# Convolutions of a forward and backward step moved beside the MLP matmuls, on one core

## The chip, the core and the metric

One NeuronCore of a Trainium2 chip: TensorE (PE) for matmuls into PSUM, VectorE (DVE), ScalarE (ACT) and GpSimd (POOL) for elementwise work, SyncE (SP) which issues transfers, and 16 DMA engines between HBM and SBUF. The metric is device time in microseconds of one execution, lower is better. All tensors are bf16.

## What is computed

A layer norm of x (2048 rows, 1024 channels), then two branches that are added to x: a gated convolution over the sequence and a gated MLP; and the gradients of all inputs but one for a given grad_out. Cut to what matters:

```python
xn = layernorm(q)                                   # [2048, 1024]
# branch A, per channel: a 4-tap shift, a product, a long convolution by FFT of length 4096
k_shift = sum(k_pad[:, t:t+S] * shift_k[:, 3-t] for t in range(4))
kv = k_shift * v
y  = irfft(rfft(kv, 4096) * rfft(ssm_k, 4096))[:S] + kv * ssm_D
A  = xn * y
# branch B, F = 3584
gate = xn @ W_gate;  up = xn @ W_up
h = relu(gate) * up;  B = h @ W_down
out = q + A + B
outputs = out, and vjp(grad_out) for q, k, v, shift_k, ssm_k, ssm_D, W_gate, W_up, W_down
```

The convolution needs, per channel, three forward transforms (of kv, of ssm_k, and of grad_out * xn), three products in the frequency domain, and three inverse transforms (of y, of the gradient of kv and of the gradient of ssm_k). The MLP needs nine products of 2048 x 1024 x 3584: gate, up, h W_down, grad of h, grad of W_down, grads of W_gate and W_up, and two products for the grad of xn.

## The kernel before

The program is recorded in Python, and a scheduler orders each engine's instructions by priority; engines run their own lists strictly in that order and wait for each other by semaphores. Buffers come from pools with a fixed number of buffers per name; an allocation waits until the oldest buffer of that name is free.

Stages, in the order in which they are written:

1. `_a_branch`, first part: tables of sines (R1, FW, IA, RB) on POOL, DVE and ACT. Beside it the layer norm: one load of x, sums, `xn_dram` and `gy_dram` (grad_out * xn) written.
2. `_a_branch`, first pass over eight groups of 128 channels (`A_load`, `A_part1`, `A_part2`): the taps on a channel-major copy (made by transposing DMAs), `fwd_transform` for kv, gy and ssm_k (matmuls with R1 at L299, evictions at L48, 64 matmuls of 128 columns with FW at L309 and L311), `jpass` (L320) to swap real and imaginary halves, products on DVE (L434 to L457), and a spill of three 1 MB forms to HBM.
3. Second pass over the same groups (`B_load`, `inverse_A`, `inverse_B`): reload of the forms, matmuls with IA (L335), 64 TensorE transposes a form (L345), matmuls with RB (L357), outputs.
4. Gate and up (L755, L759): xnT loaded by transposing DMAs; 7 column blocks of 512 by 16 row tiles; each step has 16 matmuls of 512 columns, a relu on ACT (L762), a masked product on DVE (L764), a product on POOL (L767), and three stores of 128 KB (SP and ACT queues).
5. Out (L806): per row tile a transposed load hT, 2 x 28 matmuls.
6. Per block of 512 hidden columns: the gradient of h (L837; two loads and two stores of 128 KB per row tile, on SP, ACT and POOL queues), and then, from SBUF, the gradients of W_gate and W_up (L853).
7. Gradient of W_down (L888); W_gate and W_up are transposed by two DMAs beside it (L881, L882).
8. Gradient of x (L924, L928): per row tile two transposed loads and 2 x 56 matmuls, then the layer norm's backward on DVE.

Transfers are issued from SP, ACT and POOL; all transposing DMAs from SP. Stage 4 starts when stage 3 is over, because `for _ in abr: pass` exhausts the branch first and its pools hold SBUF and PSUM until then:

```python
    next(abr)
    for _ in abr:
        pass
```

Of the kernel before, what the change touches and what calls it, by code (L numbers as in the profile page):

```python
# [21 lines left out]
def a_branch(tc, S, D, k, v, shift_k, ssm_k, ssm_D, gy_d, y_d, out_gk, out_gv, out_gsk, out_gh, out_gsD):  # L22
    with ExitStack() as ctx:
        yield from _a_branch(ctx, tc, S, D, k, v, shift_k, ssm_k, ssm_D, gy_d, y_d, out_gk, out_gv, out_gsk, out_gh,
                             out_gsD)


def _a_branch(ctx, tc, S, D, k, v, shift_k, ssm_k, ssm_D, gy_d, y_d, out_gk, out_gv, out_gsk, out_gh, out_gsD):
    nc = tc.nc
    N1 = S // P  # L30
    K1 = 2 * N1
    CL = P // N1
    NCH = N1
# [12 lines left out]

    def ev_act(out, in_):
        nc.scalar.copy(out=out, in_=in_)  # L48

    def ev_dve(out, in_):  # L50
        nc.vector.tensor_copy(out=out, in_=in_)

    _rr = [0]

    def ev_rr(out, in_):
        if _rr[0] % 3 == 2:
            nc.vector.tensor_copy(out=out, in_=in_)
        else:
            nc.scalar.copy(out=out, in_=in_)
        _rr[0] += 1  # L60

    tq = nc.sync
    dq = nc.gpsimd

    acon = ctx.enter_context(tc.tile_pool(name="acon", bufs=1))
    aps = ctx.enter_context(tc.tile_pool(name="aps", bufs=2, space=bass.MemoryType.PSUM))

    R1 = acon.tile([P, CL, 2, K1], BF16, name="R1")
    FW = acon.tile([P, K1, 3, 64], BF16, name="FW")
# [201 lines left out]
    def tm_view(ap2d):  # L271
        return ap2d.rearrange("(n1 n2) c -> n2 n1 c", n2=P)
# [716 lines left out]
```

## Time and profile before

| | us |
|---|---|
| timed, median of 3 | 3142.05 (3135.73 to 3146.0) |
| profiled execution, span from first to last instruction | 3167.4 |
| PE busy | 2355.5 (74%) |
| DVE busy | 1162.3 (37%) |
| ACT busy | 719.9 (23%) |
| DMA traffic | 422.90 MB, mean 134 GB/s |

The profiled execution's span lies 0.8% above the timed median. A busy PE counts matmuls that overlap, so it is not PE at its peak; how fast it works is seen from how far apart matmuls start. [...]

### The profile page before, as it was taken

Reading aid. Unit: us, or ns where it says so; the run is one execution under the profiler, and the core shown is the slowest. Engines: PE = TensorE matmul, PEld = TensorE weight load, DVE = VectorE, ACT = ScalarE, POOL = GpSimd, SP = SyncE. Lnnn points to the kernel's source line nnn. Section 1 sums busy time; section 2 is a strip of 40 time slices with the busy share of each in tenths; the row PEclk is TensorE's granted clock in tenths of the full one; section 3 lists DMA queues with packets and bytes.
Section 4 is the critical chain, followed back from the end, with each engine's and each line's share of the span. In section 5 each row is a group of like instructions: output and inputs, shape, how many; then the busy total and the mean of one; then the engine's idle time right before and its main releaser. Section 6 shows DMA issues by size and latency. Waiting matters only on the chain. (4 is left out here: it accounts for less than half of the span.)

```text
span 3167.4 us, 35589 instructions
## 1 busy us (share of the span) xinstructions
PE 2355.5 (74%) x14665; PEld 1256.9 (40%) x14850; DVE 1162.3 (37%) x1290; ACT 719.9 (23%) x623; POOL 417.4 (13%) x547
## 2 busy tenths in 40 slices
PE   0155655555555543599997997999999998999998
PEld 0033433334445443244443443444444443444443
DVE  9687565554655546111111122211112200122233
ACT  3255665653323321011110001111111100000000
POOL 1221111000000000233331001100011000111110
PEclk9978888777777776799998999999999998999999
DMA  1695331247688947844457767444454398254452
GB/s 63 207 187 128 94 99 60 92 121 108 129 117 113 135 99 101 248 151 159 142 160 204 161 159 228 127 121 113 105 136 131 122 192 209 77 125 117 113 124 63
DMA packets 695987, 422.90 MB, mean 134 GB/s; under 512 B 517264, under 2 KB 649872, under 8 KB 689680
## 3 DMA queue, kind: packets, MB, share of 16 engines
q1 hardware_dynamic: 568480, 221.32, 34.8%
q0 software_dynamic: 29008, 100.18, 10.6%
q10 hardware_dynamic: 98336, 99.13, 10.3%
q8 instruction: 116, 1.90, 0.3%
q14 instruction: 47, 0.39, 0.0%
HBM read 154.16 MB, written 158.35 MB: 99 GB/s over the span
## 5 line engine op out<-in xcount | busy, mean ns | idle before, releaser
L853 PEld LDWEIGHTS <-xn_nat 128*128 128x128 bf16 x1792 | 177.2, 99 | 238.9 <-issue 33.0
L755 PE MATMUL ps_g<-wg,xnT 128*128 128x512 bf16 x876 | 212.8, 383 | 79.6 <-issue 72.4
L48 ACT CAST cp<-psa 128x2048 bf16<-128x2048 f32 x96 | 174.0, 1873 | 366.2 <-PE psa L335 349.5
L853 PE MATMUL ps<-gg_blk,xn_nat 128*128 128x512 bf16 x879 | 210.0, 390 | 21.3 <-ACT wo L857 19.3
L888 PE MATMUL ps<-g_nat,hs 128*128 128x512 bf16 x878 | 199.6, 388 | 21.3 <-ACT wo L893 19.4
L806 PE MATMUL ps<-wd,hT 128*128 128x512 bf16 x878 | 197.5, 385 | 23.6 <-DMA hT<-h_dram 18.4
L759 PE MATMUL ps_u<-wu,xnT 128*128 128x512 bf16 x880 | 211.0, 380 | 0.9
L837 PE MATMUL ps<-wdT,goT 128*128 128x512 bf16 x877 | 198.2, 381 | 16.7 <-ACT gh L844 14.3
L764 DVE SCALAR_TENSOR_TENSOR upm<-rg,ps_u 128x512 bf16<-128x512 bf16 x112 | 76.9, 688 | 349.4 <-PE ps_u L759 318.1
L299 PE MATMUL ps<-R,xt_h 128*128 128x512 bf16 x128 | 47.5, 514 | 211.7 <-DVE xn_t L717 102.0
L48 ACT CAST bsb<-ps 128x2048 bf16<-128x2048 f32 x96 | 173.7, 1876 | 134.4 <-DVE prod L446 59.4
L853 PE MATMUL ps<-gu_blk,xn_nat 128*128 128x512 bf16 x878 | 201.4, 379 | 0.9
L924 PE MATMUL ps<-wgT,ggT 128*128 128x512 bf16 x879 | 197.5, 379 | 1.8 <-DVE wo L895 0.9
L928 PE MATMUL ps<-wuT,guT 128*128 128x512 bf16 x878 | 197.5, 379 | 0.9
L345 PE MATMUL pstr<-identb,cp 128*128 128x128 bf16 x1536 | 130.4, 267 | 66.1 <-ACT cp L48 59.0
L859 DVE CAST wo<-ps 128x512 bf16<-128x512 f32 x56 | 38.7, 692 | 364.8 <-PE ps L853 320.7
L309 PE MATMUL ps<-bsb,FW 128*128 128x128 bf16 x768 | 130.5, 270 | 55.9 <-ACT bsb L48 55.9
L755 PEld LDWEIGHTS <-xnT 128*128 128x128 bf16 x896 | 88.2, 99 | 186.2 <-issue 82.4
L767 POOL TENSOR_TENSOR ht<-rg,upm 128x512 bf16<-128x512 bf16 x112 | 129.0, 1152 | 250.8 <-DVE upm L764 247.5
L762 ACT ACTIVATE rg<-ps_g 128x512 bf16<-128x512 f32 x112 | 66.8, 597 | 411.7 <-PE ps_g L755 278.5
L844 ACT CAST gh<-ps 128x512 bf16<-128x512 f32 x112 | 65.4, 585 | 399.0 <-PE ps L837 275.6
L345 PEld LDWEIGHTS <-cp 128*128 128x128 bf16 x1536 | 125.6, 124 | 70.7 <-ACT cp L48 63.2
(241 smaller groups left out, 2978.4 us busy)
## 6 DMA issues: line engine op xcount, KB each, us to landing
forms_d<-prod POOLq DMA_DIRECT2D x24, 1024.0 KB, 4.3
rg_dram<-rg SPq DMA_DIRECT2D x112, 128.0 KB, 1.8
up_dram<-upm ACTq DMA_DIRECT2D x112, 128.0 KB, 1.7
rg_t<-rg_dram ACTq DMA_DIRECT2D x112, 128.0 KB, 3.8
h_dram<-ht SPq DMA_DIRECT2D x112, 128.0 KB, 1.7
upm_t<-up_dram POOLq DMA_DIRECT2D x112, 128.0 KB, 3.5
gg_dram<-gg_blk SPq DMA_DIRECT2D x112, 128.0 KB, 3.7
gu_dram<-gu_blk ACTq DMA_DIRECT2D x112, 128.0 KB, 3.1
```

Source lines behind the costliest of these rows:

```text
L48: nc.scalar.copy(out=out, in_=in_)
L309: nc.tensor.matmul(ps2[:, j * P:(j + 1) * P], lhsT=fw[:, 0:128], rhs=bsb[:, 0, k1, :], start=True, stop=False)
L345: nc.tensor.transpose(pst[:, j * P:(j + 1) * P], cpf[:, (q + j) * P:(q + j + 1) * P], identb[:])
L755: nc.tensor.matmul(ps_g[:], lhsT=xnT[:, kt, st * P:(st + 1) * P], rhs=wg[:, kt, :], start=(kt == 0), stop=(kt == DT - 1))
L759: nc.tensor.matmul(ps_u[:], lhsT=xnT[:, kt, st * P:(st + 1) * P], rhs=wu[:, kt, :], start=(kt == 0), stop=(kt == DT - 1))
L767: nc.gpsimd.tensor_tensor(out=ht[:], in0=rg[:], in1=upm[:], op=ALU.mult)
L806: nc.tensor.matmul(ps[:], lhsT=hT[:, kt, :], rhs=wd[:, kt, ob * 512:(ob + 1) * 512], start=(kt == 0), stop=(kt == FT - 1))
L837: nc.tensor.matmul(ps[:], lhsT=goT[:, kt, st * P:(st + 1) * P], rhs=wdT[:, kt, :], start=(kt == 0), stop=(kt == DT - 1))
L853: nc.tensor.matmul(ps2[:], lhsT=xn_nat[:, skt, dc * P:(dc + 1) * P], rhs=blk[:, skt, :], start=(skt == 0), stop=(skt == ST - 1))
L888: nc.tensor.matmul(ps[:], lhsT=hs[:, skt, j * P:(j + 1) * P], rhs=g_nat[:, skt, ob * 512:(ob + 1) * 512], start=(skt == 0), stop=(skt == S ...
L924: nc.tensor.matmul(ps[:], lhsT=ggT[:, kt, :], rhs=wgT[:, kt, ob * 512:(ob + 1) * 512], start=(i == 0), stop=(i == n_mm - 1))
L928: nc.tensor.matmul(ps[:], lhsT=guT[:, kt, :], rhs=wuT[:, kt, ob * 512:(ob + 1) * 512], start=(i == 0), stop=(i == n_mm - 1))
```

## The change

The file is rewritten around two classes.

**ABranch** does the convolution. Per group of 128 channels it does everything in one pass, nothing is spilled: a sequence of 2048 is read as 128 x 16 (natural layout, 256 B pieces), the transform is a 32-point step (matmuls with R, 16 of 512 columns for two halves), a transposition of 32 x 32 blocks on DVE (`flip`), and a 64-point step (32 matmuls of 128 columns with FW). Products (`cmul`) are complex multiplications by parts on DVE. The inverse runs the same steps backwards. The taps use natural-layout rows with an offset, so the transposing DMAs of the branch are gone; the 4 x 128 sums of the shift gradient are now matmuls with a selecting matrix (`hsel`).

**LnMlp** does layer norm and MLP. The layer norm runs in chunks of 1, 1, 2, 4, 4, 4 row tiles, with sums on ACT, and transposes on PE into 16 tiles that stay in SBUF. Gate/up works on hidden blocks of 256 and pairs of row tiles: matmuls of 256 columns, two row tiles in one PSUM bank; the product that POOL did is on DVE. The order of phases is now gate/up, grad_hidden, grad_down (W_down), grad_in (W_gate, W_up), out, grad_x. grad_hidden stores its two results and grad_in loads them back in slabs of 512 KB. Out comes after grad_in; its phase also transposes W_gate and W_up, in eight slices. Tiles come from small pools shared by all phases: 16 of 2 KB, 5 of 4 KB (weights and slabs), 9 of 1 KB (steps), 4 PSUM banks; the branch has 2 x 2 banks. Every transfer is issued from SP.

The branch's instructions get priorities of their own: its matmuls and loads stand ahead of the MLP, its evictions, DVE work and stores behind it. Core of the diff:

```diff
-    next(abr)
-    for _ in abr:
-        pass
...
+PR_LN = -10_000_000
+PR_A_PE = 0
+PR_A_LD = 0
+PR_B = 10_000_000
+PR_A_EV = 20_000_000
...
+    def flip(self, src):
+
+        dst = self.big.tile([P, NB1, P], BF16, name="flp", tag="big")
+        df = dst[:].rearrange("p k c -> p (k c)").bitcast(F32).rearrange("p (k cp) -> p cp k", cp=64)
+        sf = src[:].rearrange("p cp r i -> p (cp r i)").bitcast(F32).rearrange("p (cp r) -> p cp r", cp=64)
+        for c0 in range(0, 64, 32):
+            self.pri.at(PR_A_EV)
+            self.nc.vector.transpose(out=df[:, c0:c0 + 32, :], in_=sf[:, c0:c0 + 32, :])
+        return dst
+
+    def forward(self, src, form_name, add_D=None):
+        B = self.big.tile([P, 64, NB1, 2], BF16, name="B", tag="big")
+        for u in range(2):
+            for j in range(2):
+                ps = self.ps.tile([P, 1024], F32, name="ps1", tag="aps")
+                for jj in range(2):
+                    r0 = 8 * j + 4 * jj
+                    self.mm(ps[:, 512 * jj:512 * jj + 512], self.R[:, u].rearrange("p h a k -> p (h a k)"),
+                            src[:, r0:r0 + 4, :].rearrange("p r c -> p (r c)"))
+                t0 = 16 * u + 8 * j
+                self.act(B[:, :, t0:t0 + 8, :], ps[:].rearrange("p (r cp i) -> p cp r i", r=8, i=2))
+        Bf = self.flip(B)
+        F = self.frm.tile([P, 2, 16, P], BF16, name=form_name, tag="frm")
+        for k0 in range(0, NB1, 8):
+            ps = self.ps.tile([P, 8, P], F32, name="ps2", tag="aps")
+            for j in range(8):
+                self.mm(ps[:, j, :], self.FW[:, k0 + j].rearrange("p a k -> p (a k)"), Bf[:, k0 + j, :])
...
+                for w, name in ((wg, "ps_g"), (wu, "ps_u")):
+                    ps = self.ps_tile(name)
+                    for s in range(2):
+                        xT = self.xnT[2 * sp + s]
+                        for kt in range(self.DT):
+                            nc.tensor.matmul(ps[:, s * 256:s * 256 + 256], lhsT=xT[:, kt * P:(kt + 1) * P],
+                                             rhs=w[:, kt, :], start=(kt == 0), stop=(kt == self.DT - 1))
+                    pss.append(ps)
+                rg, up, ht = self.ev_tile("rg"), self.ev_tile("up"), self.ev_tile("ht")
...
+            for sp in range(self.ST // 2):
+                rg, up = self.ev_tile("rgl"), self.ev_tile("upl")
+                fl = lambda t: t[:].rearrange("p s f -> p (s f)")
+                nc.sync.dma_start(out=fl(rg), in_=rg_d[hb, sp])
+                nc.sync.dma_start(out=fl(up), in_=up_d[hb, sp])
...
+                gh = self.ev_tile("gh")
+                nc.scalar.copy(out=fl(gh), in_=ps[:])
+                nc.vector.tensor_tensor(out=up[:], in0=gh[:], in1=up[:], op=ALU.mult)
+                nc.vector.tensor_tensor(out=gh[:], in0=gh[:], in1=rg[:], op=ALU.mult)
+                rows = slice(sp * 256, sp * 256 + 256)
+                nc.sync.dma_start(out=gg_d[rows, cols].rearrange("(s p) f -> p s f", p=P), in_=up[:])
+                nc.sync.dma_start(out=gu_d[rows, cols].rearrange("(s p) f -> p s f", p=P), in_=gh[:])
...
+            if st < 8:
+                w, wT = (Wg, self.wgT) if st < 4 else (Wu, self.wuT)
+                c = (st % 4) * 256
+                nc.sync.dma_start_transpose(out=wT[:, :, c:c + 256], in_=w[c:c + 256, :])
...
+    a.run()
+    a.close()
+    tc.cur_priority = PR_B
+    b.gate_up(B_W_gate, B_W_up, rg_d, up_d, h_d)
+    b.grad_hidden(B_W_down, g, rg_d, up_d, gg_d, gu_d)
+    b.grad_down(g, h_d, out_9)
+    b.open_right(B_W_down)
+    b.grad_in(xn_d, gg_d, gu_d, out_7, out_8)
+    b.close_left()
+    b.out_phase(x, xn_d, y_d, h_d, B_W_gate, B_W_up, out_0[0])
+    b.grad_x(g, xn_d, y_d, gg_d, gu_d, out_1[0])
```

How the instructions stand now, at three places. First PE in gate/up. Before, a run of gate or up matmuls holds nothing else (ps_g, ps_u: PSUM of gate and up):

```order
L755 LDWEIGHTS xnT
L755 MATMUL ps_g<-wg,xnT 128x512
L759 LDWEIGHTS xnT
L759 MATMUL ps_u<-wu,xnT 128x512
L759 LDWEIGHTS xnT
```

Now, in the same phase, PE goes to the first transform of kv of the first group (kvt, matrix R, L63) and back:

```order
L525 LDWEIGHTS xnT
L525 MATMUL ps_g<-wg,xnT 128x256
L63 LDWEIGHTS R
L63 MATMUL ps_780<-kvt,R 128x512
L63 LDWEIGHTS R
L63 MATMUL ps_780<-kvt,R 128x512
L525 LDWEIGHTS xnT
```

Two matmuls of the branch stand between MLP matmuls here; elsewhere some 40 MLP matmuls stand where the branch waits for a transposition on DVE; a group's 281 matmuls and transposes of the branch are spread over some 600 to 900 of the MLP.

Second, DVE in gate/up. Before, the 112 masked products are all that DVE does in the phase, and they stand in one row, between the convolution's last row and the out phase:

```order
L577 CAST gskb<-gskf 128x4
L764 SCALAR_TENSOR_TENSOR upm<-rg,ps_u 128x512 x112
L808 TENSOR_TENSOR o_12562<-ps,xa 128x512 x2
L800 TENSOR_TENSOR xa<-xa,xn_e 128x1024
L801 TENSOR_TENSOR xa<-xa,x_e 128x1024
```

Now (up and ht: the MLP's step; t, GH, flp, C: products and a transposition of the branch):

```order
L531 SCALAR_TENSOR_TENSOR up<-rg,ps_u 128x512
L71 TENSOR_TENSOR GH<-t_962 64x1024
L533 TENSOR_TENSOR ht<-rg,up 128x512
L71 TENSOR_TENSOR GH<-t_963 64x1024
L71 TENSOR_TENSOR GH<-t_962 64x1024
L71 TENSOR_TENSOR GH<-t_963 64x1024
L292 STREAM_TRANSPOSE flp<-C 128x32x32
L531 SCALAR_TENSOR_TENSOR up<-rg,ps_u 128x512
L292 STREAM_TRANSPOSE flp<-C 128x32x32
L533 TENSOR_TENSOR ht<-rg,up 128x512
```

Both the MLP's step and the branch now stand in one list, the MLP's two instructions with one to five of the branch between them.

Third, SP in the gradient of h. Before, SP holds the stores of one result (the other and the loads are on ACT and POOL) and the transposed weights:

```order
L847 DMA gg_dram<-gg_blk 128x512 x15
L827 DMA_TRANSPOSE wdT<-in_B_W_down_dram 128x8x512
L847 DMA gg_dram<-gg_blk 128x512
L861 DMA out_dram<-wo 128x512 x8
L847 DMA gg_dram<-gg_blk 128x512 x15
```

Now (rgl, upl: the loads; gg_d, gu_d: the stores; ghn: a store of the branch):

```order
L566 DMA gg_d<-upl 128x2x256
L567 DMA gu_d<-gh 128x2x256
L553 DMA rgl<-rg_d 128x512
L554 DMA upl<-up_d 128x512
L553 DMA rgl<-rg_d 128x512
L554 DMA upl<-up_d 128x512
L553 DMA rgl<-rg_d 128x512
L554 DMA upl<-up_d 128x512
L83 DMA out_dram<-ghn 128x2048
L566 DMA gg_d<-upl 128x2x256
L549 DMA_TRANSPOSE wdT<-in_B_W_down_dram 128x8x256
L567 DMA gu_d<-gh 128x2x256
```

Loads and stores of three steps alternate in one list, with the branch's stores and the transposed weights between them.

## Rows read from the trace of the kernel before

**Rows 1.** The page: busy tenths of PE in 40 slices of the span.

```profile
PE   0155655555555543599997997999999998999998
```

**Rows 2.** Busy time by stretch: from:to, length, engines (instructions), granted clock, DMA share, GB/s.

```profile
165.00:680.00 515.00, 294.19 (x2097) 187.35 (x2119) 334.71 (x201) 309.14 (x170) 63.61 (x109) 0.82 0.45 112
680.00:1265.00 585.00, 282.38 (x4576) 266.82 (x4575) 315.84 (x227) 174.05 (x96) 42.81 (x52) 0.75 0.71 114
...
1333.00:1722.00 389.00, 386.28 (x1764) 175.81 (x1798) 74.27 (x108) 63.23 (x106) 124.01 (x109) 1.00 0.50 158
...
2770.00:3167.00 397.00, 385.10 (x1757) 175.25 (x1792) 116.30 (x161) 0.00 (x0) 43.21 (x33) 0.99 0.44 108
```

**Rows 3.** Chain of work that ended last: start, length, engine, line, count.

```profile
2782.63 6.04 PE ps L924 x28
2794.72 6.04 PE ps L924 x28
```

**Rows 4.** Timeline of PE, first pass: start, length of one, line, shape; 16 rows left out.

```profile
412.10 0.22 PE L309 MATMUL ps<-bsb,FW 128*128 128x128 bf16 x1
...
413.05 0.22 PE L311 MATMUL ps<-bsb,FW 128*128 128x128 bf16 x1
```

**Rows 5.** Groups by line and shape, DVE: count, busy us, mean ns, idle before.

```profile
L764 DVE SCALAR_TENSOR_TENSOR upm<-rg,ps_u 128x512 bf16<-128x512 bf16 x112 | 76.9, 688 | 349.4 <-PE ps_u L759 318.1 <-ACT rg L762 15.2 <-remote 11.1
L845 DVE TENSOR_TENSOR gu_blk<-gh,rg_t 128x512 bf16<-128x512 bf16 x112 | 47.6, 425 | 139.8 <-ACT gh L844 118.7 <-DMA rg_t<-rg_dram 21.1
L457 DVE TENSOR_TENSOR prod<-prod,ptmp 64x4096 bf16<-64x4096 bf16 x8 | 18.3, 2289 | 0.3
L801 DVE TENSOR_TENSOR xa<-xa,x_e 128x1024 bf16<-128x1024 bf16 x16 | 11.0, 691 | 0.5
L411 DVE TENSOR_TENSOR kv_tm<-kshift_tm,v_tm 128x2048 bf16<-128x2048 bf16 x8 | 9.8, 1222 | 4.9 <-DMA kshift_tm<-kshT 4.7
L179 DVE TENSOR_TENSOR t<-n2v_f,m_f 128x1024 f32<-128x1024 f32 x4 | 4.8, 1211 | 0.0
```

**Rows 6.** The same view, ACT.

```profile
L693 ACT ACTIVATE sq<-d_all 128x1024 bf16<-128x1024 bf16 x16 | 16.3, 1048 | 9.6 <-DVE var_f L694 9.6
L114 ACT ACT_TABLE_LOAD x1 | 1.3, 1283 | 0.7 <-PEq L973 0.7
L48 ACT CAST sDb<-psb 128x1024 bf16<-128x1024 f32 x1 | 1.0, 1012 | 4.1 <-PE psb L256 4.1
```

**Rows 7.** Timeline of PE: first convolution matmul and first gate/up matmul.

```profile
112.34 1.01 PE L299 MATMUL ps<-R,xt_h 128*128 128x512 bf16 x2 [102.00 <-DVE xn_t L717]
1299.72 0.58 PE L755 MATMUL ps_g<-wg,xnT 128*128 128x512 bf16 x1 [72.22 <-issue]
```

**Rows 8.** Busy time by stretch (columns of rows 2), gradient of h in two blocks.

```profile
2017.00:2065.00 48.00, 46.09 (x209) 20.61 (x211) 13.55 (x34) 10.53 (x18) 8.59 (x16) 1.00 0.85 204
...
2200.00:2245.00 45.00, 41.39 (x187) 18.48 (x189) 13.20 (x34) 9.95 (x17) 8.60 (x16) 1.00 0.93 218
```

**Rows 9.** DMA issues: queue, operation, count, KB each, median us to landing.

```profile
rg_t<-rg_dram ACTq DMA_DIRECT2D x112, 128.0 KB, 3.8
gg_dram<-gg_blk SPq DMA_DIRECT2D x112, 128.0 KB, 3.7
y_dram<-y_tm POOLq DMA_DIRECT2D x8, 512.0 KB, 5.1
```

**Rows 10.** Timeline of SP's issues: start, length of the issue.

```profile
1502.38 0.34 SPq L772 DMA_DIRECT2D h_dram<-ht  x1
2548.78 43.58 SPq L881 DMA_TRANSPOSE wgT<-in_B_W_gate_dram  x1
2643.02 5.46 SPq L910 DMA_TRANSPOSE ggT<-gg_dram  x1
```

**Rows 11.** SP's waits: who waited for whom, us in total, times, longest.

```profile
SPq L290 <- PE ps L299: 259.3, 12, 46.2
SPq L366 <- PE psa L335: 147.7, 14, 47.3
```

More of the change, by code (lines that the diff above doesn't have):

```diff
@@ L726 @@
-    lnb.release()
-    next(abr)
-    for _ in abr:
-        pass
-    L, R = "left", "right"
-    gq_dma = nc.gpsimd
-    p_xnT = tc.alloc_tile_pool(name="gf_xnT", bufs=1, side=L)
-    p_w = tc.alloc_tile_pool(name="gf_w", bufs=2, side=L)
-    p_ev1 = tc.alloc_tile_pool(name="gf_ev", bufs=3, side=L)
-    p_ps1 = tc.alloc_tile_pool(name="gf_ps", bufs=2, space=bass.MemoryType.PSUM)
-    xnT = p_xnT.tile([P, DT, S], BF16, name="xnT")
-    for kt in range(DT):
-        nc.sync.dma_start_transpose(out=xnT[:, kt, :], in_=xn_dram[:, kt * P:(kt + 1) * P])
@@ L862 @@
-    p_ps3b.release()
-    p_ps3.release()
-    p_ev3b.release()
-    p_ev3.release()
-    p_blk.release()
-    p_wdT.release()
-    p_res3.release()
-    p_hs = tc.alloc_tile_pool(name="b2_hs", bufs=3, side=R)
-    p_ev4 = tc.alloc_tile_pool(name="b2_ev", bufs=3, side=R)
-    p_ps4 = tc.alloc_tile_pool(name="b2_ps", bufs=2, space=bass.MemoryType.PSUM)
-    p_w5 = tc.alloc_tile_pool(name="b5_w", bufs=1, side=L)
-    wgT = p_w5.tile([P, FT, D], BF16, name="wgT")
-    wuT = p_w5.tile([P, FT, D], BF16, name="wuT")
@@ L876 @@
-    for fc2 in range(0, FT, 2):
-        hs = p_hs.tile([P, ST, 2 * P], BF16, name="hs")
-        eng = nc.scalar if (fc2 // 2) % 2 == 0 else gq_dma
-        eng.dma_start(out=hs[:], in_=_r(h_dram[:, fc2 * P:(fc2 + 2) * P], "(t p) f -> p t f", p=P))
-        if fc2 == min(2, (FT - 1) // 2 * 2):
-            nc.sync.dma_start_transpose(out=wgT[:], in_=B_W_gate[:, :])
-            nc.sync.dma_start_transpose(out=wuT[:], in_=B_W_up[:, :])
-        for j in range(2):
-            fc = fc2 + j
-            for ob in range(DB):
-                ps = p_ps4.tile([P, 512], F32, name="ps")
-                for skt in range(ST):
-                    nc.tensor.matmul(ps[:], lhsT=hs[:, skt, j * P:(j + 1) * P],
-                                     rhs=g_nat[:, skt, ob * 512:(ob + 1) * 512],
-                                     start=(skt == 0), stop=(skt == ST - 1))
-                wo = p_ev4.tile([P, 512], BF16, name="wo")
-                if ob % 2 == 0:
-                    nc.scalar.copy(out=wo[:], in_=ps[:])
-                else:
-                    nc.vector.tensor_copy(out=wo[:], in_=ps[:])
-                (nc.scalar if ob % 2 == 0 else gq_dma).dma_start(
-                    out=out_9[fc * P:(fc + 1) * P, ob * 512:(ob + 1) * 512], in_=wo[:])
@@ L954 @@
-    p_ps5.release()
-    p_sm5.release()
-    p_ev5.release()
-    p_gT.release()
-    p_w5.release()
+    assert S % 256 == 0 and D == 1024 and F % 256 == 0
+    x, g = A_q[0], grad_out[0]
+    dram = ctx.enter_context(tc.tile_pool(name="dram", bufs=1, space=bass.MemoryType.DRAM))
+    xn_d = dram.tile([S, D], BF16, name="xn_d")
+    y_d = dram.tile([S, D], BF16, name="y_d")
+    rg_d = dram.tile([F // 256, S // 256, P, 512], BF16, name="rg_d")
+    up_d = dram.tile([F // 256, S // 256, P, 512], BF16, name="up_d")
@@ new lines @@
+    h_d = dram.tile([S, F], BF16, name="h_d")
+    gg_d = dram.tile([S, F], BF16, name="gg_d")
+    gu_d = dram.tile([S, F], BF16, name="gu_d")
+    pri = Pri(tc)
+    b = LnMlp(tc, pri, S, D, F)
+    a = ABranch(tc, pri, S, D, A_k[0], A_v[0], g, A_shift_k, A_ssm_k, A_ssm_D, xn_d, y_d, out_2[0], out_3[0], out_4,
+                out_5, out_6)
+    b.open_left()
+    a.open()
+    tc.cur_priority = PR_LN
+    b.layer_norm(x, xn_d, a.frm, "frm", a.tmp, "tmp", a.sm)
+    a.tables()
+    a.run()
+    a.close()
```

1343 lines of the change are left out of this document (569 added, 774 removed).

## Prediction

> **What bounds the kernel now.** I read the slices of the page first: PE is half idle for the first 16 of 40 slices and nearly full after [rows 1]. The table by stretches says why. From 165 to 680 us (first convolution pass) PE is busy 294 of 515 us, DVE 335, ACT 309; from 680 to 1265 us (second pass) PE 282, DVE 316; the granted clock is 0.82 and 0.75. From 1333 us on PE is busy 386 of 389 us in gate/up and 385 of 397 us in the last stage, at 1.00 and 0.99 [rows 2]. The first gate/up matmul starts at 1299.7 us [rows 7]. So the program is two programs end to end: 1300 us in which no engine is the bound and three hand work to each other, and 1867 us bound by PE.
>
> The PE part has a floor. Two pieces of 28 matmuls of 512 columns follow each other every 6.045 us (56 in 12.09) [rows 3]: 0.2159 us each. The MLP has 8,064 such matmuls: 1741 us. So the 1867 us hold some 126 us of stalls, and what the change can win is in the 1300 us.
>
> **The change, step by step.** The convolution leaves the front of the program and is put between the MLP matmuls. Its PE work doesn't vanish, it is added to 1741 us.
>
> *PE.* 128-column matmuls, each with its own weight load, start 17 apart in 0.95 us, 0.0559 us each [rows 4]. With 0.2159 us for 512 columns that is 0.417 ns a column plus 2.5 ns, so 0.109 us for the new 256-column ones; halving the width costs nothing by this. [...] A group of 128 channels has 24 + 33 matmuls of 512 columns (0.2159), 192 of 128 and 16 transposes (0.0559), 32 of 64 (at most 0.0559): 25.7 us. Eight groups: 205 us.
>
> *DVE per group.* 64 two-input bf16 instructions of 1024 elements at 0.691 (those on 64 partitions cost the same per element: 64x4096 takes 2.289): 44.2. Fourteen of 2048 at 1.222: 17.1. Four additions out of PSUM and twelve 32x32 transposes of 1024 f32 each: no row shows a transpose; the ends are 0.69 and 2.29, I take 1.21, that of an f32 instruction of the same size: 19.4. Small ones: 3. Sum 84 us [rows 5]. [...] *ACT per group*: 50 casts of 1024 at 1.01 [rows 6]: 51 us, never the bound.
>
> *The stages.* The order of PE puts 4.7 groups into gate/up, 2.0 into grad_hidden and 1.3 into grad_down, which ends with 451 matmuls after the last one of the convolution. From there on it is the MLP alone.
>
> Start. Gate/up needs all 16 layer-norm tiles. ACT has 32 passes at 1.05, 11 table loads at 1.28, and some 20 us of sines and casts: 68 us [rows 6]; DVE about as much. I take 85; before, the first convolution matmul came at 112 us [rows 7], and that is the upper end, 70 the lower.
>
> Gate/up. PE: 3,584 x 0.109 = 391, and 4.7 x 25.7 = 121: 512 us. DVE: 112 x (0.688 + 0.425) = 125 [rows 5], and 4.7 x 84 = 395: 520 us. Two in-order engines with the same load, woven by a fixed order: perfect cover gives 520. The other end is the first pass of before, where the busiest engine worked 335 of 515 us, 65% [rows 2]: 800. Here the gaps hold MLP matmuls, so I take a point nearer the lower end: 590.
>
> Grad_hidden. PE 195 + 52 = 247 us, DVE 266. But each of 112 steps moves four pieces of 128 KB (two in, two out): 58.7 MB, and 7.3 MB of W_down and 4.2 MB of grad_out pass through transposing DMAs. In the two stretches of before with the same traffic the DMA engines were 85 and 93% busy at 204 and 218 GB/s [rows 8], full would be about 0.24 MB/us: 293 us. Before, the tail of this was hidden behind the weight-gradient matmuls that follow in each block; now the phase runs in one piece. The convolution adds seven 0.5 MB transfers in 256 B pieces per group, at most 4 to 5 us each (a store of this form lands in 5.1 us [rows 9]), 35 us a group: 71. Sum 364 us, more than PE and DVE. From the other side: SP issues six loads, then six stores, then six loads; an issue takes 0.34 to 0.4 us [rows 10], a load lands after 3.8 us, a store after 3.7 [rows 9], so a round of three steps is about 2.4 issue + 3.8 + ACT and DVE 2 + the next issue 1 to 2, or 10 us: 112/3 x 10 = 373. I take 385. The lower end is 300 (a quarter higher rate), the upper 480.
>
> Grad_down. 896 x 0.2159 = 193, and 33 of the convolution; then 4.2 MB of the next operand must land in tiles that only now come free, 17 us at the rate above less 3 hidden by the last sum: 240. Grad_in: 391 + 14 = 405, since no convolution is left and three buffers are ahead.
>
> Out phase. PE 193 us, 12.1 per row tile. Its transposed loads share SP's queue with W_gate and W_up, which must now be transposed in eight slices here: one whole matrix took 43.6 us of SP [rows 10], so 10.9 a slice, plus 5.5 for the tile's own and 4.4 for four pieces of 256 KB: 20.8 us against 12.1. Three tiles are loaded ahead, so about five tiles wait 8.7 us: 239. Grad_x: 387, as before, and 8 for a tail: 395.
>
> Sum: 85 + 590 + 385 + 240 + 405 + 239 + 395 = 2339 us. That stands against the profiled span of 3167.4 us, which lies above the timed median, 3142.05; by that ratio (0.992) 2320 us.
>
> What covers the removed time: some 205 us of PE, 670 us of DVE and 410 us of ACT of the convolution run in time in which PE works for the MLP. What is late next is DVE in gate/up, then the DMA engines in grad_hidden.
>
> **The rivals.**
> *The convolution sets the pace* (chance 0.2). A group is a chain: cast, transposing on DVE, matmul, cast. If nothing of one group overlaps itself, a group takes 84 + 51 + 25.7 = 161 us, and with the MLP's DVE share of 27 (125 over 4.7 groups) 188, where full DVE alone would take 111. For: single buffers for three of the loads, a few of everything else, DVE and ACT in order. Against: DVE's order shows three products of a group behind each other with nothing to wait for. Half of this excess in all eight, 77 x 8 x 0.5 = 308 us, less the 70 that gate/up has already above 520: 2577, timed 2556 us.
> *All is hidden* (0.14). Gate/up at 520, grad_hidden at 300, start at 75, out phase at 200: 2339 - 70 - 85 - 10 - 39 = 2135, or 2118 timed. For: before, gate/up kept PE busy 386 of 389 us with DVE beside it [rows 2]. Against: both loads in gate/up are level.
> *SP's one queue stops everything* (0.04, slower). All 1,460 transfers now stand in one queue, where a store of the convolution that isn't ready holds the MLP's loads and stores behind it, and through their buffers ACT, DVE and PE. Waits of SP behind the convolution reached 46 and 47 us before [rows 11]. Beside the MLP, two of these per group, uncovered, add 16 x 47 = 750 us: 3090; from 2.3 per group on the change loses, and three give 3450. Against: the order puts those stores where their data is due.
> *The change doesn't do what it says* (0.02): the woven order alone doesn't make PE busy; if every handover waits, gate/up to grad_down take what the two passes took before (1100 us) beside 780 us of MLP, and the total is about 3140, no change.
> Forecast as summed: 0.6.
>
> **How the numbers follow.** The forecast's own ends are its unknowns: gate/up 540 to 700, grad_hidden 320 to 450, out phase 200 to 270, not all at one end: 2220 to 2480. The range reaches to the rivals beside it on both sides until 2 in 10 are left out: 2190 to 2560. A measurement of this kernel tells 0.3% (some 9 us) from no change. Faster: 0.6 + 0.2 + 0.14 and a little of the fourth: 0.94; within 0.3%: 0.01; slower: 0.05.
>
> **What would show it.** First gate/up matmul at 75 to 110 us. DVE over 85% busy in gate/up, and PE over 80%. The 256-column matmuls starting every 0.109 us. A transpose on DVE near 1.2 us: at 2.29 the 96 of them cost 104 us more. In grad_hidden DMA share over 0.85 and PE about 65% busy. SP waiting in the out phase on W_gate and W_up. After the last convolution matmul PE busy over 93%. Wrong it is if a group takes over 150 us, or if grad_hidden is not bound by transfers.

## The result and the profile after

The changed kernel takes 2510.07 us (median of four runs, 2500.66 to 2515.33) against 3144.03 us before: a ratio of 0.798, 95% interval 0.795 to 0.800. A median of before differs by up to 11 us between the chips of the runs below; "us off" there is the difference of two medians, and the ratios give the same within 6 us. The forecast was 2320 us with a range of 2190 to 2560. Sign and range hold; the point is 190 us, 8%, too low, and the rival "the convolution sets the pace" (2556 us) lies nearer to the measured time than the forecast does.

The page of after, busy tenths of two engines and the granted clock (PEclk, in tenths of TensorE's full speed) in 40 slices (PE stood as [rows 1] before):

```profile
PE   2784977868588657756778989999999999999998
...
DVE  7784866868578257636757300000000221323323
...
PEclk9897989989899888988889999999999999999999
```

The first 23 slices, in which the convolution runs, are neither full on PE nor on DVE; behind them PE is full. The stretches of after by stage (from:to, length, busy us of PE, PEld, DVE, ACT, POOL with instructions, granted clock, DMA share, GB/s; they answer to [rows 2]):

```profile
0.00:81.70 81.70, 24.51 (x186) 18.84 (x188) 64.78 (x212) 66.00 (x96) 4.33 (x16) 0.90 0.63 180
81.70:796.20 714.50, 551.71 (x4908) 443.60 (x4934) 505.10 (x684) 327.07 (x354) 3.72 (x9) 0.92 0.53 118
796.20:1211.00 414.80, 276.78 (x2330) 220.31 (x2338) 235.57 (x400) 165.07 (x202) 1.23 (x3) 0.86 0.78 178
1211.00:1505.30 294.30, 246.46 (x1298) 117.13 (x1322) 127.69 (x154) 110.42 (x124) 0.83 (x2) 0.92 0.64 157
1505.30:1904.10 398.80, 394.74 (x3585) 350.24 (x3584) 0.00 (x0) 65.52 (x112) 0.00 (x0) 1.00 0.40 117
1904.10:2103.20 199.10, 194.45 (x881) 87.92 (x898) 39.16 (x59) 0.58 (x1) 0.00 (x0) 0.99 0.92 214
2103.20:2498.90 395.70, 385.20 (x1758) 175.21 (x1792) 118.12 (x273) 0.00 (x0) 0.00 (x0) 0.99 0.46 113
```

| stage | forecast us | measured us | MLP without the convolution (run e1) |
|---|---|---|---|
| start | 85 | 82 | 59 |
| gate/up | 590 | 715 | 391 |
| grad_hidden | 385 | 415 | 305 |
| grad_down | 240 | 294 | 206 |
| grad_in | 405 | 399 | 397 |
| out | 239 | 199 | 201 |
| grad_x and tail | 395 | 396 | 395 |

In the span the miss is 160 us, and all of it lies in the three stages that hold the convolution (1215 forecast, 1424 measured); the out phase gave 40 us back. The other 30 us come from the step from span to timed median: the forecast took 19 us off by the ratio that before had shown, and in after the median lies 11 us above the span of the profiled execution. Who let PE wait, over the whole span of after (engine, line waited for: us, times, longest):

```profile
PE ps L63 <- DVE flp L292: 116.5, 47, 17.1
PE ps L63 <- DVE hT L75: 59.4, 7, 22.9
PE ps_h L559 <- ACT gh L562: 51.6, 21, 12.4
PE ps_sk L63 <- ACT ghn L67: 33.9, 7, 8.4
...
PE pst L281 <- ACT ghn L67: 22.9, 7, 3.9
PE ps L63 <- ACT H L67: 17.6, 7, 14.0
```

No full engine is among them. gh is the MLP's own cast in grad_hidden, and the line left out is the layer norm's at the start (30 us); the others are steps of the convolution: the transposed tiles (flp), the first tile of a group (hT), the last cast of the group before (ghn). Two of those instructions have a price that no row of before showed (groups by line and shape: count, busy us, mean ns, idle before):

```profile
L292 DVE STREAM_TRANSPOSE flp<-B 128x1024 f32<-128x1024 f32 x48 | 89.6, 1911 | 37.5 <-ACT B L67 37.4
...
L67 ACT CAST ghn<-ps 128x1024 bf16<-128x1024 f32 x16 | 72.7, 4787 | 36.5 <-PE ps L63 19.3 <-DMA out_dram<-gv 17.3
...
L67 ACT CAST C<-ps 128x1024 bf16<-128x1024 f32 x96 | 93.2, 1024 | 47.7 <-PE ps L63 47.1
```

The transpose takes 1.91 us, not 1.21; the cast that closes a group takes 4.79 us where a cast of the same size takes 1.02.

Theory after this reading: each group of the convolution puts some 65 us on PE's queue (the table's last two columns), of which 26 are its own matmuls and most of the rest is PE standing at matmuls whose operand isn't there yet. The rivals: the group's chain of handovers sets the pace (then a faster group makes a faster kernel); or single engines or transfers bind (DVE in gate/up, the DMA engines in grad_hidden).

### The profile page after: what moved, and what is told of

Same layout as the page of the kernel before. It is cut to its first block, busy times and chain, and to the rows that moved or that the text cites. A ratio compares the mean times of both kernels' runs of the same rounds, so it can differ in the third digit from the quotient of the medians.

```text
span 2498.9 us, 36518 instructions
## 1 busy us (share of the span) xinstructions
PE 2073.8 (83%) x14931; PEld 1413.2 (57%) x15050; DVE 1090.4 (44%) x1778; ACT 734.7 (29%) x889; POOL 10.1 (0%) x30
## 5 line engine op out<-in xcount | busy, mean ns | idle before, releaser
L525 PEld LDWEIGHTS <-xnT 128*128 128x128 bf16 x3584 | 351.9, 99 | 76.5 <-issue 23.8
L559 PE MATMUL ps_h<-wdT,goT 128*128 128x256 bf16 x1792 | 227.9, 287 | 51.7 <-ACT gh L562 51.6
L525 PE MATMUL ps_g<-wg,xnT 128*128 128x256 bf16 x1792 | 233.3, 277 | 0.1
L525 PE MATMUL ps_u<-wu,xnT 128*128 128x256 bf16 x1792 | 231.0, 276 | 0.2
L596 PE MATMUL ps_d<-g_nat,hs 128*128 128x512 bf16 x870 | 206.5, 389 | 19.2 <-DMA hs<-h_d 12.6
L615 PE MATMUL ps_w<-ggs,xn_nat 128*128 128x256 bf16 x1792 | 201.4, 274 | 4.1 <-DMA xn_nat<-xn_d 3.5
L662 PE MATMUL ps_o<-wd,hT 128*128 128x512 bf16 x878 | 194.6, 381 | 4.7 <-DMA hT<-h_d 3.7
L693 PE MATMUL ps_x<-wgT,ggT 128*128 128x512 bf16 x879 | 197.6, 379 | 0.9
L693 PE MATMUL ps_x<-wuT,guT 128*128 128x512 bf16 x877 | 197.3, 379 | 0.9
L615 PE MATMUL ps_w<-gus,xn_nat 128*128 128x256 bf16 x1792 | 197.9, 273 | 0.0
L63 PE MATMUL ps<-flp,FW 128*128 128x128 bf16 x768 | 58.7, 228 | 82.1 <-DVE flp L292 51.8
```

The costliest lines, as they stand in the source:

```text
L63: self.nc.tensor.matmul(out, lhsT=lhsT, rhs=rhs, start=start, stop=stop)
L525: nc.tensor.matmul(ps[:, s * 256:s * 256 + 256], lhsT=xT[:, kt * P:(kt + 1) * P], rhs=w[:, kt, :], start=(kt == 0), stop=(kt == self.DT - 1))
L559: nc.tensor.matmul(ps[:, s * 256:s * 256 + 256], lhsT=xT[:, kt * P:(kt + 1) * P], rhs=w[:, kt, :], start=(kt == 0), stop=(kt == self.DT - 1))
L596: nc.tensor.matmul(ps[:], lhsT=hs(st)[:, j * P:(j + 1) * P], rhs=gn[st][:, ob * 512:ob * 512 + 512], start=(st == 0), stop=(st == self.ST ...
L615: nc.tensor.matmul(ps[:, d * 256:d * 256 + 256], lhsT=xn[st][:, dc * P:(dc + 1) * P], rhs=sl(st), start=(st == 0), stop=(st == self.ST - 1))
L662: nc.tensor.matmul(ps[:], lhsT=hT[:, kt, :], rhs=self.wd[:, kt, oc], start=(kt == 0), stop=(kt == self.FT - 1))
```

## The experiments

### The two halves apart

e1 leaves the convolution out, e2 the MLP:

```diff
# e1_mlp_alone
-    a.tables()
-    a.run()
     a.close()
...
                 nc.sync.dma_start(out=xn_d[st * P:(st + 1) * P, :], in_=xt[:, j, :])
+                nc.sync.dma_start(out=self.y_d[st * P:(st + 1) * P, :], in_=xt[:, j, :])
# e2_conv_alone
     a.close()
     tc.cur_priority = PR_B
+    b.close_left()
+    b.ps.release()
+    b.per.release()
+    return
     b.gate_up(B_W_gate, B_W_up, rg_d, up_d, h_d)
```

> Leaves the whole convolution out (no tables, no groups; y is filled with the normalized rows, so five outputs are not written). Theory A, the groups of the convolution set the pace of the first three stages: without them gate/up falls to its PE floor, 3,584 x 0.109 = 391 us and at most 410; grad_hidden to about 300 us if the DMA engines bound it, to 350 to 375 us if the round of six loads and six stores in SP's queue bounds it as the prediction had it; grad_down to 205. Total about 1,900 to 1,960 us. Theory B, the stages of the MLP have waits of their own (SP's queue, buffers), which the convolution only fills: gate/up stays above 470 us and grad_hidden above 385 us, total above 2,050 us.

> Leaves the MLP out from gate/up on (layer norm, tables and the eight groups are left). In the changed kernel a group takes 172 us. Theory A, a group is a chain of handovers that needs this time by itself: 140 to 165 us a group, end at 1,200 to 1,350 us. Theory B, the group is slow because its instructions stand behind MLP work in five in-order queues: alone it takes 100 to 120 us (DVE's own work is about 92 us of it), end at 880 to 1,020 us.

e1 takes 1956 us (one execution, as for e2); its stages are the last column of the table above. The three stages that hold the convolution in after (columns as above), and PE's only wait of size in grad_hidden:

```profile
59.30:450.60 391.30, 391.30 (x3588) 350.74 (x3586) 124.34 (x224) 66.28 (x111) 0.00 (x0) 1.00 0.60 174
450.60:755.80 305.20, 223.98 (x1795) 184.28 (x1793) 91.03 (x218) 64.38 (x110) 0.00 (x0) 0.92 0.87 231
755.80:961.30 205.50, 196.03 (x879) 88.28 (x897) 3.31 (x8) 33.73 (x58) 0.00 (x0) 0.98 0.46 136
```

```profile
PE ps_h L560 <- ACT gh L563: 79.0, 48, 4.5
```

e2 takes 1105 us. The cast of yt in e2 (min/median/max ns, first and last start), two per group, the same in after, what PE waits for in e2, and the stretch of e2's groups, counting line 63 alone (the convolution's matmuls; from:to, length, busy us of PE and PEld, granted clock, DMA share, GB/s):

```profile
L67 ACT CAST yt<-ps x16: 1012/1013/1013, 147.0 to 1044.5; 128x1024 bf16<-128x1024 f32 x16
```

```profile
L67 ACT CAST yt<-ps x16: 1012/1012/1012, 157.7 to 1360.0; 128x1024 bf16<-128x1024 f32 x16
```

```profile
PE ps L63 <- DVE flp L292: 380.5, 47, 19.8
```

```profile
62.00:1103.50 1041.50, 366.84 (x2215) 209.44 (x2247) 0.58 0.31 36
```

First to last yt is seven groups and a little: 897 / 7 = 128 us a group, where after has 1202 / 7 = 172. That lies between the two theories (140 to 165 and 100 to 120). The granted clock is 0.58 in e2's stretch, and line 63 is busy 367 us there, 263 in after, 13 us a group more: by this estimate the chain alone would be somewhat shorter than 128 us at the clock of after. So the MLP's stages are as the prediction had them without the convolution (gate/up 391, grad_hidden 305 against 293, with a DMA share of 0.87 and 231 GB/s), and a group alone is slower than DVE's work in it (the prediction's 84 us, 92 with the transposes at 1.91) and faster than the sum of its steps (161 in the prediction). The difference between the kernel and e1 is 2499 - 1955 = 544 us of span for eight groups: 22 at the start, 323 in gate/up, 110 in grad_hidden, 89 in grad_down. The last three are 522 us, 65 a group. By the rows of e1 and after, PE is busy 264 of them (1075 against 811 us) and stands 258: 33 and 32 us a group. The group's own 25.7 at the full clock are 205 of the 264; the remaining 58, 7 a group, fit the lower granted clock (0.92, 0.86 and 0.92 in the three stages).

### The group's last cast

```diff
-        dv = dst[:, 0:16, :].rearrange("p r c -> p (r c)").rearrange("p (q n) -> p n q", n=NB1)
+        dv = dst[:, 0:16, :].rearrange("p r c -> p (r c)").rearrange("p (q n) -> p q n", n=NB1)
-            self.act(dv[:, n0:n0 + 16, :], ps[:])
+            self.act(dv[:, :, n0:n0 + 16], ps[:].rearrange("p n q -> p q n"))
```

> The cast that closes a group (ghn) writes runs of 16 neighbouring elements instead of single elements 64 bytes apart; the order on every engine is unchanged. In the changed kernel it takes 4.8 us, sixteen of them 73 us of ACT; with runs it should take about 1.0 us as the casts of C do, 60 us of ACT less. Theory A, the group's chain sets the pace and this cast is in it: 45 to 60 us off the total (PE waits for ghn sum to 57 us), 2,450 to 2,465 us. Theory B, ACT has room (29% busy) and the cast is off the path: under 15 us, 2,495 us or more.

2479.5 us (ratio 0.788, 0.785 to 0.791): 30 us off, between the two theories. The cast and PE's waits in e3:

```profile
L67 ACT CAST ghn<-ps x16: 1012/1015/1018, 189.1 to 1373.2; 128x1024 bf16<-128x1024 f32 x16
```

```profile
PE ps L63 <- DVE hT L75: 84.5, 7, 22.2
...
PE ps_sk L63 <- ACT ghn L67: 10.0, 3, 5.1
```

The waits for ghn fall from 57 to 11 us, but those for hT, which comes next, rise from 59 to 84: half of the gain met the next late operand. The cast is on the path, and so is what stands behind it.

### The price of the transpose

```diff
# e4_flip_price
-            self.nc.vector.transpose(out=df[:, c0:c0 + 32, :], in_=sf[:, c0:c0 + 32, :])
+            self.nc.vector.tensor_tensor(out=df[:, c0:c0 + 32, :], in0=sf[:, c0:c0 + 32, :],
+                                         in1=sf[:, c0:c0 + 32, :], op=ALU.max)
# e5_flip_rows: flip, for all tiles but that of the inverse of GH
-        df = dst[:].rearrange("p k c -> p (k c)").bitcast(F32).rearrange("p (k cp) -> p cp k", cp=64)
+        df = dst[:].rearrange("p k c -> p (k c)").bitcast(F32).rearrange("p (cp k) -> p cp k", cp=64)
-        return dst
+        return dst[:].rearrange("p k c -> p (k c)").rearrange("p (cp k i) -> p k cp i", cp=64, i=2)
```

> The 96 transposes on DVE (1.91 us each) become an f32 maximum of the tile with itself, of the same shape with the same reads and writes, so the convolution's values are wrong; the order on every engine is unchanged. Price expected 1.21 us, as the prediction took for the transpose: 67 us of DVE less. Theory A, the mis-sized transpose is in the chain and cost what it was too small by: 50 to 67 us off, 2,443 to 2,460 us. Theory B, DVE has room (71% busy in gate/up) and it costs nothing: under 15 us. If the strided write is what makes it slow, the maximum also takes about 1.9 us and the run tells nothing on the time.

> Five of a group's six transposed tiles (80 of 96 instructions) are written by DVE in rows of 32 neighbouring f32 elements instead of elements 256 bytes apart, and the matmuls read the tile with a stride instead. The order of the engines is planned anew with it. Theory A, the price of the transpose is in the group's chain: 80 x about 0.7 us = 56 us of DVE less and 40 to 70 us off the 2,510 us (PE's waits on these instructions sum to 116 us). Theory B, what a group gains is taken by its other handovers: 0 to 15 us. If TensorE pays for the strided reads, the 640 matmuls of 128 columns (58.7 us busy with the rest of their line) take longer than their 0.22 us each, and the time may rise.

e4: a plain maximum with the same reads and writes takes the same 1.9 us, and the time stays (2500.6 us, ratio 0.795, 0.791 to 0.798). The price belongs to the write pattern, single f32 elements 256 bytes apart, not to transposing.

```profile
L292 DVE TENSOR_TENSOR flp<-B x48: 1877/1906/1954, 69.0 to 1321.9; 128x1024 f32<-128x1024 f32 x48
```

e5: 2480.3 us (ratio 0.789, 0.786 to 0.792), 30 us off, between the two theories. By form, in e5 (C's mean mixes 32 instructions in rows and 16 as before), then PE's matmuls on them in e5, and last the same in after:

```profile
L293 DVE STREAM_TRANSPOSE flp<-C 128x1024 f32<-128x1024 f32 x48 | 68.3, 1453 | 36.4 <-ACT C L67 36.4
L293 DVE STREAM_TRANSPOSE flp<-B 128x1024 f32<-128x1024 f32 x48 | 57.9, 1229 | 39.8 <-ACT B L67 39.6
```

```profile
L63 PE MATMUL ps<-flp,FW 128*128 128x128 bf16 x768 | 97.0, 287 | 45.1 <-DVE flp L293 24.3 <-ACT H L67 15.6 <-DVE ln_s L496 5.1
```

```profile
L63 PE MATMUL ps<-flp,FW 128*128 128x128 bf16 x768 | 58.7, 228 | 82.1 <-DVE flp L292 51.8 <-ACT H L67 17.6 <-DVE ln_s L493 6.3
```

Written in rows, the transpose takes the 1.23 us that the prediction had taken from an f32 instruction of its size. DVE is 53 us shorter, PE reads with a stride and is busy 38 us longer on these matmuls and 16 on those with RB (57.7 against 41.2), and yet the kernel gains 30 us, since PE waits 70 instead of 117 us for the tiles. That isn't what a PE-bound or a DVE-bound stage does.

### Buffers and queues at a group's end

```diff
# e6_cast_slots: e3_cast_runs and
-        self.ts = self.pool("a_ts", 3, side=R)
+        self.ts = self.pool("a_ts", 4, side=R)
-        self.w4 = tc.alloc_tile_pool(name="b_w4", bufs=5, side="left")
+        self.w4 = tc.alloc_tile_pool(name="b_w4", bufs=4, side="left")
-        dg = self.sm.tile([P, 4, P], BF16, name="dg", bufs=1)
+        dg = self.tmp.tile([P, 4, P], BF16, name="dg", tag="tmp")
# e7_own_queue: def store
-        self.nc.sync.dma_start(out=out, in_=in_)
+        self.nc.gpsimd.dma_start(out=out, in_=in_)
# e9_three_mends: e6_cast_slots and e7_own_queue
```

> The cast of run e3_cast_runs, and four buffers instead of three for the tiles in time order (hT, kvt, yt, gkv, gv, gks, gk, ghn), paid for with four instead of five weight tiles of the MLP and a shared buffer for dg. Theory A, the next group's start waits for a buffer that the last store of the group before holds (in e3_cast_runs PE waits 84 us for hT, 7 times): these waits fall under 30 us and the time to 2,420 to 2,445 us. Theory B, DVE comes late to hT anyway, because its own queue is behind: waits for hT stay above 60 us, time 2,465 to 2,490 us.

> All stores of the convolution (and the shift of gks by one partition) are issued from GpSimd, which is idle, instead of SP. Theory A, a store of the convolution is late because SP's queue stands before others' waits (the shift of gks went out 17 us after its data were there, and DVE waits 50 us for it in total; ghn's stores let hT wait 31 us): DVE's waits on these fall under 30 us, 30 to 60 us off, 2,450 to 2,480 us. Theory B, the time is set by DVE and ACT handovers, and the queue does not matter: within 15 us of 2,510. Theory C, a queue of GpSimd is slower with pieces of 256 B, and its stores land later: slower than 2,525 us.

> The cast in runs, the fourth buffer and the own queue of the convolution's stores together (alone: cast 30 us off, cast and buffer 64, queue 40). Theory A, each of them takes a different wait at the end of a group, and the gains add: 64 + 40 = 104 us off 2,510, about 2,405 us. Theory B, they shorten the same wait (the next group's start), and the later one finds it gone: 2,430 to 2,450 us.

e6: 2446.0 us (ratio 0.778, 0.776 to 0.781), 64 us off, 34 of them by the changed buffers and the order that is planned anew with them (8 by an earlier start: gate/up begins at 74 us, in e3 at 83). hT is gone from PE's waits; what is late instead, in e6:

```profile
PE ps L63 <- DVE flp L292: 131.7, 48, 13.4
PE ps_h L559 <- ACT gh L562: 69.0, 26, 14.6
PE ps_sk L63 <- DVE dg L251: 37.5, 8, 14.9
```

e7: 2470.2 us (0.786, 0.783 to 0.789), 40 us off, theory A: PE waits 2 instead of 59 us for hT, while its waits for ghn rise from 57 to 75 and those for gh from 52 to 70. e9, all three: 2465.9 us (0.783, 0.780 to 0.785), no better than e6 alone and outside both theories. The mends don't add. In e9 grad_down starts late, for a load in SP's queue:

```profile
PE ps_d L596 <- DMA g_nat<-in_grad_out_dram: 33.2, 2, 20.1
```

In e6 that wait is 2.6 us, so it is larger than what e9 lies above e6 (20 us by the medians, 13 by the ratios). Why this load comes late when the stores leave SP's queue isn't settled.

### Grad_hidden with two buffers a step

```diff
-                nc.scalar.copy(out=fl(gh), in_=ps[:])
-                nc.vector.tensor_tensor(out=up[:], in0=gh[:], in1=up[:], op=ALU.mult)
-                nc.vector.tensor_tensor(out=gh[:], in0=gh[:], in1=rg[:], op=ALU.mult)
+                nc.vector.tensor_tensor(out=fl(up), in0=ps[:], in1=fl(up), op=ALU.mult)
+                nc.vector.tensor_tensor(out=fl(rg), in0=ps[:], in1=fl(rg), op=ALU.mult)
+                gh = rg
```

> In grad_hidden both products read TensorE's sums directly and write over the loaded tiles, so a step needs two buffers instead of three (9 buffers hold 4.5 steps instead of 3) and ACT's 112 casts (66 us) are left out; DVE has about 112 x 2 x 0.27 = 60 us more (the products take 0.69 instead of 0.42 us). In the changed kernel the stage takes 415 us, with the DMA engines 78% busy; without the convolution 303 us with 85%. Theory A, the round trip of the buffers through SP's queue sets the stage (PE waits 52 us for gh's buffer, DVE 115 us for loads): 350 to 385 us. Theory B, the chain of the two convolution groups sets it (2 x 128 us of their own beside the MLP): 400 us or more, DMA share not above 0.80. Theory C, DVE's load decides: longer than 430 us.

2504.1 us (0.797, 0.794 to 0.800): no change in all, and no theory's range: grad_hidden takes 315 us. The stretches of e8 from grad_hidden to grad_in, counting line 63 alone (the convolution's matmuls), below the same of after, and last the cast of yt in e8:

```profile
790.70:1106.00 315.30, 7.27 (x79) 4.53 (x80) 0.90 0.84 229
1106.00:1457.10 351.10, 80.33 (x711) 48.44 (x715) 0.93 0.49 95
1457.10:1906.30 449.20, 13.93 (x125) 8.87 (x128) 0.97 0.49 136
```

```profile
796.30:1213.40 417.10, 58.77 (x504) 35.88 (x514) 0.86 0.78 179
1213.40:1505.50 292.10, 47.63 (x409) 28.91 (x409) 0.92 0.64 156
1505.50:1904.30 398.80, 0.00 (x0) 0.00 (x0) 1.00 0.40 117
```

```profile
L67 ACT CAST yt<-ps x16: 1012/1012/1018, 158.1 to 1477.2; 128x1024 bf16<-128x1024 f32 x16
```

The newly planned order put only 79 instead of 504 of them into grad_hidden; the rest moved behind, and the three stages together take 1116 against 1108 us. Over the three stages together the convolution costs the same, though a group now takes 1319 / 7 = 188 us: the kernel's time doesn't follow the length of a group. With hardly any of the convolution in it, grad_hidden has a DMA share of 0.84, and two buffers a step (315 us) are no faster than e1's three (305), which speaks against the buffers' round trip as its limit; with two groups in it, the share is 0.78.

### The convolution first

```diff
-PR_A_EV = 20_000_000
+PR_A_EV = 5_000_000
```

> One number changed: the casts, products and stores of the convolution come before those of the MLP where both are ready (PR_A_EV 5e6 instead of 20e6). A group takes 172 us in the changed kernel and 128 us with no MLP beside it. Theory A, a group is slow because its steps stand behind MLP steps in the queues of ACT, DVE and SP, and TensorE waits for them: a group falls to 140 to 155 us, TensorE's waits for transposed tiles (116 us) by half, 60 to 100 us off. Theory B, the MLP's own casts then come late, its four banks of sums run full, and TensorE waits for these: within 30 us of 2,510 or slower. Theory C, the queues' order is already near ready-time order and the number changes little: within 10 us.

2729.4 us (0.866, 0.863 to 0.868): 219 us slower than the changed kernel. yt, gate/up (columns as in the table by stage) and PE's waits in e11:

```profile
L67 ACT CAST yt<-ps x16: 1012/1012/1012, 145.8 to 1078.8; 128x1024 bf16<-128x1024 f32 x16
```

```profile
81.80:1229.50 1147.70, 701.63 (x5860) 535.80 (x5905) 783.83 (x1007) 506.13 (x512) 5.79 (x14) 0.80 0.49 92
```

```profile
PE ps L63 <- DVE flp L292: 262.7, 43, 20.8
PE ps_h L559 <- ACT gh L562: 75.9, 48, 4.0
PE ps_g L525 <- ACT rg L530: 41.3, 13, 13.4
```

Theory B has the sign, but its own waits, for the MLP's steps in gate/up, are the smaller part (41 us for ps_g, 22 for ps_u). A group now takes 933 / 7 = 133 us, nearly as fast as alone, so the steps do stand behind the MLP's in the queues, as theory A said. But the kernel doesn't get faster, it loses 219 us. The convolution comes to an end within gate/up, which takes 1148 us, and PE waits 263 instead of 117 us for transposed tiles: all eight groups now share gate/up's 3,584 matmuls, 448 a group (49 us of PE) where after has some 800, so between two steps of a group there are fewer MLP matmuls, and PE stands at the next step of the group. PE stands 446 us in this stage, and its granted clock is 0.80 (0.92 in after); of the 231 us that the three stages lose, 184 are standing and 47 longer busy. What follows it shows in the same run: grad_hidden without the convolution takes 302 us and grad_down 205, as in e1.

### The best version

```diff
# e10_mends_and_rows: e9_three_mends with the rows of e5_flip_rows
# e12_slots_and_rows: e6_cast_slots with the rows of e5_flip_rows
```

> e9_three_mends with the transposed tiles in rows of e5_flip_rows (30 us off by itself: 55 us of DVE less, about 55 us of TensorE more). Theory A, after the mends DVE and its handovers are still what TensorE waits for: another 25 to 40 us off against e9_three_mends. Theory B, with the waits at a group's end gone the added TensorE work counts in full: no gain or up to 30 us lost.

> e6_cast_slots (2,446 us, the fastest so far, stores left in SP's queue) with the transposed tiles in rows of e5_flip_rows. Theory A, TensorE's waits for these tiles (132 us in e6_cast_slots) are a term of their own, which the cheaper writes shorten (from 117 to 70 us in e5_flip_rows) at 55 us of added TensorE time: 2,415 to 2,430 us. Theory B, every order planned anew falls out by chance some 20 us better or worse, as e9_three_mends (2,466 us, though it holds all of e6_cast_slots and the queue that gained 40 us by itself) suggests: anywhere from 2,430 to 2,470 us.

e10: 2456.9 us (0.780, 0.776 to 0.783), 9 us under e9, not told apart from it. e12: 2420.9 us (0.770, 0.767 to 0.772), 89 us, 3.5%, under the changed kernel and the fastest of all, in theory A's range. The same rows gain 30 us on after, 9 on e9 and 25 on e6, so chance in the order, theory B, isn't excluded as a part of it. In e12:

```profile
PE ps L63 <- DVE flp L293: 79.6, 42, 10.5
PE ps_h L562 <- ACT gh L565: 68.0, 22, 15.8
PE ps_sk L63 <- DVE dg L251: 40.7, 8, 15.2
```

The waits for the tiles fall from 132 in e6 to 80 us. What is left are still handovers: of these tiles, of gh's buffers and of dg at a group's start.

## Why the prediction was right, and where it was wrong

**The floor and the stages without the convolution** were right but for the out phase: MLP stages of 391, 305, 206, 397, 201 and 395 us in e1 against terms of 391, 293, 207, 405, 239 and 395. The price of 256-column matmuls (0.109 us) holds: 3,584 in 391 us. That the convolution's DVE and ACT work would run beside the MLP was right too: 634 us were won.

**The range** held, but not by the forecast's own terms: their ends were 2220 to 2480, and 2510 lies above them; it is inside because the range was drawn out to the rival at 2556. One of the two signs for "wrong" was a group of over 150 us, and it took 172.

**The cover of a group** is the step that failed. The prediction gave the three stages 313 us over what e1 measures for the MLP alone, 39 a group, by taking "a point nearer the lower end" in gate/up, 70 us above the 520 of perfect cover. Measured are 522 there (and 22 at the start). In gate/up, the 323 us fall on 1,256 recorded matmuls of the convolution, at 281 a group (its 16 transposes apart) 4.5 groups: PE's own work 4.5 x 25.7 = 115; 46 more in which PE is busy (552 us where 391 + 115 would do at 1.00), put down to the clock, granted at 0.92 (at 0.50 from 156.64 to 159.20 us, where six matmuls of 512 columns follow each other every 0.43 us, and at 1.00 from 167.96 to 169.69, where seven follow every 0.25); standing, 714.5 - 551.7 = 163. The prediction had no term for the clock. The reason given for the lower end, that the gaps of before now hold MLP matmuls, holds for PE only if these stand ahead of the late step in its queue; at a step that is late PE stands, however much MLP work is behind it (47 times and 116.5 us for the transposed tiles in after).

**DVE's load** wasn't the bound: 505 of 714 us busy (71%), not over 85%, and PE 77%, not over 80%. The transpose at 1.91 instead of 1.21 us (96 x 0.7 = 67 us) was inside the ends given, and e5, e10 and e12 show what it is worth: 9 (not told apart from nothing) to 30 us net of PE's strided reads. The cast at 4.79 us wasn't seen at all: the prediction priced all 50 of a group at 1.01; it is worth 30 us (e3).

**Grad_hidden** came near (415 for 385), on wrong grounds: without the convolution the stage takes 305 with the DMA engines 87% busy, SP's round of 10 us per three steps (373) isn't there in e1 or e8, and what makes 415 of it are two groups of the convolution at 55 to 60 us. With a DMA share of 0.78 the prediction's other sign for "wrong" is there.

**The out phase** was too dear by 40 us, for a mis-sized term. The prediction took 10.9 us of SP for a slice of the transposed weights and a round of 20.8. SP's issues in after:

```profile
1949.05 8.02 SPq L654 DMA_TRANSPOSE wuT<-in_B_W_up_dram  x1
1957.16 4.35 SPq L633 DMA_TRANSPOSE hT<-h_d  x1
1961.56 0.58 SPq L648 DMA_DIRECT2D xe<-xn_d  x1
1963.61 8.01 SPq L654 DMA_TRANSPOSE wuT<-in_B_W_up_dram  x1
```

A slice takes 8.0, a round 14.6 us against PE's 12.1; the tiles loaded ahead cover that, and PE waits 3.7 us for hT in the whole stage.

**The rivals.** "The convolution sets the pace" named a group of 188 us and 2556 us; 172 and 2510 came. Part of its mechanism is borne out. The chain alone takes up to 128 us (e2), and the MLP's own steps in gate/up, 124 us of DVE and 66 of ACT in e1, stand in the same two queues: over 4.5 groups 28 and 15 us a group, with the chain up to 171. That sum is an estimate that no run tests by itself, but e11, which lets the group's steps go first, brings a group down to 133. What the runs don't bear out is that the kernel's time follows the length of a group: with 133 us it loses 219 us (e11), with 188 us it loses nothing (e8). In both runs the order was planned anew, so they don't vary the chain alone. What the runs show stands between forecast and rival: every step of the chain that comes later than the planned order has it costs PE its lateness, and mending one moves part of it to the next (ghn to hT, hT to dg and gh). "All hidden" fell with gate/up at 715 us instead of 520, "SP's one queue" cost 40 us (e7), not 750, and "the change doesn't do what it says" fell with the 634 us. In the rival of SP's queue two numbers don't follow from its own 47 us a wait: the change loses from 2.2 stores a group, not 2.3, and three give 3467 us in the span in which two give 3090, not 3450.

What stays open: how much of e9's loss is the queue and how much the order that is planned anew with each edit; e3 and e4 alone kept the order of after.

## What to carry to other kernels

When a chain of small steps is woven by a fixed order into the work of a full engine, price it as the full engine's own work plus its waits at each handover, and not by the load of the engines beside it: here 65 us a group where its matmuls took 26, 32 of them standing. Hastening the chain can lose where the order then holds less other work between its steps (133 instead of 172 us a group, 219 us slower); what helps is that each operand is there before its turn: cheaper instructions just ahead of a matmul, one more buffer where a group hands over to the next. Before pricing an instruction by its size, look at how far apart its elements are written: here 4.79 against 1.02 us for casts of one size, 1.91 against 1.23 for transposes.

## What the hardware showed that was not expected

ACT's cast of 1024 elements took 1.015 us when it wrote runs of 16 bf16 (e3, though it then read PSUM with a stride) and 4.79 us when it wrote single ones 64 bytes apart (after). DVE's 1024 f32 took 1.23 us in rows (e5) and 1.9 us with elements 256 bytes apart, transposed or not (after, e4); the 1.23 us lie near the 1.211 us of the f32 instruction of that size from which the prediction took its price [rows 5]. TensorE's 768 matmuls on the transposed tiles were busy 97.0 us when they read pairs of bf16 128 bytes apart (e5), 58.7 us when they read neighbouring ones (after). All three measurements agree in direction; why elements further apart take longer, no run here shows.

Matmuls of 128 columns with their own weights follow each other every 0.063 us in after (16 from 442.69 to the next at 443.70, at a granted clock of 1.00), where the prediction took 0.0559 us from before [rows 4]:

```profile
442.69 1.17 PE L63 MATMUL ps<-Y,IA 128*128 128x128 bf16 x16
443.70 0.71 PE L525 MATMUL ps_u<-wu,xnT 128*128 128x256 bf16 x5
```
